# Attention feeding a two-layer FFN: tails loaded last, token order written into PSUM, zeros in early waits, casts in landing order

**Chip and metric.** One core of one Trainium2 chip. Times are device microseconds (us) of whole executions. Every run quoted fell in the same (fast) state. A run of one kernel spreads by about 1%.

## The reference, cut to what matters

```python
# q, k, v: (8 batches, 8 heads, 576 tokens, 64) fp32
scores = q @ k.T / 8, only where |query - key| <= 32, softmax over keys
x = (softmax @ v).transpose(0, 2, 1, 3).reshape(4608, 512)    # tokens x (heads*64)
out = gelu_tanh(x @ w_in) @ w_out                             # 512 -> 2048 -> 512
```

## The kernel before

Attention of one batch is woven between the matmuls of the feed-forward network of a block of 512 tokens. `ffn_in` is the input projection (`mm`/`ph <- xT,w_in` in the profile), then comes the output projection (`mm <- w_out,gT`). The heads of a pair sit on 64 partitions each. Queries are held four to a position: token 4p+j stands at column (j, p). So scores, weights and values come out with all tokens of j = 0 first, then j = 1 and so on, but the projection wants `xT` in token order, (p, j). A *group* is one pair of heads over 480 tokens of a batch (512 in batch 0); a fifth group holds the last tokens, the *tails*, of all pairs. The parts concerned, with cuts marked by "...":

```python
def weigh(b, g):                          # values and denominators of one group
    o = psO.tile([128, 512], FP32, name="ps_o")      # PSUM
    d = psO.tile([128, 512], FP32, name="ps_d")      # PSUM
    for i, (hf, pr, k0, c, p0, p1, off) in enumerate(todo):
        ...
        for w, bk in ((0, o), (1, d)):
            for h in range(2):            # the two heads of the pair
                nc.tensor.matmul(
                    bk[r0:r0 + 64, at:at + 4 * n].rearrange(
                        "d (j p) -> d j p", j=4)[:, :, p0 - q0:p1 - q0],
                    V[:, c, 2 * pr + h, :] if w == 0 else ones,
                    pes[hf][:, h, off:off + 4 * (p1 - p0)].rearrange("k (j p) -> k j p", j=4),
                    start=(i == 0), stop=(i == len(todo) - 1), ...)

def invert(b, g, d):                      # 1/denominator on ScalarE: exp(-ln d)
    nc.scalar.activation(lt[:, 0:n], d[:, 0:n], AF.Ln)
    nc.scalar.activation(lt[:, 0:n], lt[:, 0:n], AF.Exp, scale=-1.0)

def spread(b, g, o, lt):                  # the "product", on VectorE: token order is made here
    o4, l4 = (x[:, 0:n].rearrange("d (j p) -> d j p", j=4) for x in (o, lt))
    ...
    nc.vector.tensor_tensor(
        xT[:, g, pos:pos + 4 * e].rearrange("d (p j) -> d j p", j=4),   # fp16, step of 4 elements
        o4[:, :, p:p + e], l4[:, :, p:p + e], op=ALU.mult)

# loads of batch 1, in order: q,k of heads 0-1; q and k tails (tokens 512-575); q,k of heads 2-7;
# w_out 0, then halves of w_out 1-3 with v heads 0-5 between them (the v tail after v head 1), v heads 6-7
# casts on GpSimd while block 0 runs: w_out 1, v pairs 0 and 1, w_out 2, w_out 3, v pairs 2 and 3
# spin(n, width): matmuls of zeros, meant to keep TensorE's clock up; spin(4, 256) in the opening
```

The softmax here doesn't subtract the row's maximum and nothing guards it: scores larger than these inputs give would overflow.

## Time and profile before

| | before |
|---|---|
| timed median (3 runs first, 4 beside the changed kernel) | 329.77, 330.17 us |
| span of the profiled execution | 330.8 us |
| second input projection (block 1) starts | 67.96 us |
| from there to the end | 262.8 us |

Two views of the page of the kernel before follow. The first line gives each engine's busy time, its share of the span and its number of instructions. The second is the chain of work that ended last, by engine and line.

```profile
PE 314.4 (95%) x2244; PEld 152.4 (46%) x2244; DVE 149.2 (45%) x292; ACT 200.6 (61%) x314; POOL 57.5 (17%) x81
...
PE mm L445 37%; PE mm L432 22%; PE ph L432 13%; PE ps_o L377 4%; PE ps_s L344 4%; PE ps_d L377 3%; DMA KT<-k 2%; DMA vr<-in_v_dram 2%; DMA kr<-in_k_dram 2%; DVE xT L403 1%; SPq L123 1%; DVE pe L359 1%; SPq L132 1%; SPq L304 1%; ACT lt L392 1%
```

Nearly the whole chain is TensorE (PE). The value and denominator matmuls (`ps_o`, `ps_d`, L377) hold only 7% of it and the product (`xT`, L403, on DVE) 1%.

### The profile page before, as it was taken

The numbers are of one execution on the slowest core, as the hardware profiler recorded it, in microseconds if no ns is written. First come the engines' busy times: TensorE is split into PE (matmuls) and PEld (weight loads), VectorE is DVE, ScalarE is ACT, GpSimd is POOL, SyncE is SP. The second block draws the span as 40 slices with busy tenths as digits, with TensorE's granted clock in tenths as the row PEclk, the third lists the DMA queues.
The fourth block names the chain that finished last, engine by engine and source line by source line (L and its number), as shares of the span: only waits on it lengthen the run. The fifth ranks groups of instructions, "written<-read, shape, count | busy, mean of one in ns | idle before, by whom it ended". The sixth has DMA issues, their size and how long they took to land.

```text
span 330.8 us, 5704 instructions
## 1 busy us (share of the span) xinstructions
PE 314.4 (95%) x2244; PEld 152.4 (46%) x2244; DVE 149.2 (45%) x292; ACT 200.6 (61%) x314; POOL 57.5 (17%) x81
## 2 busy tenths in 40 slices
PE   7669987999999999999999999999999999999994
PEld 3543543544454445444544454445444554444441
DVE  5585575680468046814581457235632650210011
ACT  1476573467766677667767766685768567705600
POOL 3652345292104010401040104010000000000000
PEclk9698997999999999999999999999999999999999
DMA  7999999699979698979899899979161100020012
GB/s 196 275 361 303 329 316 292 175 155 152 231 179 141 122 205 170 124 134 206 176 103 135 179 218 91 152 191 208 65 119 26 65 37 28 0 95 34 0 63 63
DMA packets 119722, 50.57 MB, mean 153 GB/s; under 512 B 100144, under 2 KB 111152, under 8 KB 119696
## 3 DMA queue, kind: packets, MB, share of 16 engines
q1 hardware_dynamic: 88096, 45.10, 55.8%
q0 software_dynamic: 31520, 4.98, 20.0%
q8 instruction: 17, 0.28, 0.4%
q10 hardware_dynamic: 80, 0.13, 0.1%
q14 instruction: 9, 0.07, 0.1%
HBM read 37.62 MB, written 9.44 MB: 142 GB/s over the span
## 4 chain that ended last, share of the span: by engine, by line
PE 85%; DMA 5%; SPq 3%; DVE 3%; ACT 1%; POOL 1%; issue 1%; POOLq 0%
PE mm L445 37%; PE mm L432 22%; PE ph L432 13%; PE ps_o L377 4%; PE ps_s L344 4%; PE ps_d L377 3%; DMA KT<-k 2%; DMA vr<-in_v_dram 2%; DMA kr<-in_k_dram 2%; DVE xT L403 1%; SPq L123 1%; DVE pe L359 1%; SPq L132 1%; SPq L304 1%; ACT lt L392 1%
## 5 line engine op out<-in xcount | busy, mean ns | idle before, releaser
L445 PE MATMUL mm<-w_out,gT 128*128 128x512 f16 x576 | 134.9, 382 | 2.9 <-POOL w_out L183 2.2
L432 PE MATMUL mm<-xT,w_in 128*128 128x512 f16 x364 | 90.1, 382 | 1.3 <-DVE xT L403 1.3
L432 PEld LDWEIGHTS <-w_in 128*128 128x128 f16 x576 | 56.3, 98 | 69.6 <-issue 4.2
L445 PEld LDWEIGHTS <-gT 128*128 128x128 f16 x576 | 53.0, 98 | 66.5 <-issue 4.7
L436 ACT ACTIVATE gT<-mm 128x512 f16<-128x512 f32 x91 | 54.2, 597 | 38.4 <-PE mm L432 37.8
L403 DVE TENSOR_TENSOR xT<-ps_o,lt 128x480 f16<-128x480 f32 (+5 forms) x38 | 37.1, 1018 | 43.0 <-ACT lt L392 43.0
L432 PE MATMUL ph<-xT,w_in 128*128 128x512 f16 x212 | 55.9, 381 | 0.0
L391 ACT ACTIVATE lt<-ps_d 128x480 f32<-128x480 f32 (+3 forms) x40 | 22.2, 554 | 48.8 <-PE ps_d L377 48.7
L350 ACT ACTIVATE pe<-ps_s 128x704 f16<-128x704 f32 x64 | 43.3, 727 | 10.0 <-PE ps_s L344 9.0
L412 DVE TENSOR_TENSOR xT<-ps_o,lt 128x384 f16<-128x384 f32 (+1 forms) x8 | 7.9, 987 | 81.1 <-ACT lt L392 81.1
L449 DVE COPY yo<-mm 128x512 f32<-128x512 f32 x36 | 24.8, 690 | 34.1 <-PE mm L445 34.0
L436 ACT ACTIVATE gT<-ph 128x512 f16<-128x512 f32 x53 | 31.6, 596 | 13.0 <-PE ph L432 13.0
L359 DVE TENSOR_TENSOR pe<-pe,mask 128x704 f16<-128x704 f16 x64 | 33.1, 547 | 5.9 <-ACT pe L350 5.4
L163 POOL DMA_DIRECT2D V<-in_v_dram x24 | 23.2, 980 | 63.9 <-PE ps_o L377 47.6
L377 PEld LDWEIGHTS <-V 128*64 128x64 f16 x336 | 19.3, 114 | 18.7 <-issue 15.5
L392 ACT ACTIVATE lt<-lt 128x480 f32<-128x480 f32 (+3 forms) x40 | 23.5, 587 | 1.3
L377 PE MATMUL ps_d<-pe,ones 128*64 128x192 f16 (+2 forms) x264 | 23.8, 244 | 0.0
L377 PE MATMUL ps_o<-pe,V 128*64 128x160 f16 (+2 forms) x244 | 22.7, 248 | 0.7 <-DVE pe L359 0.4
L344 PE MATMUL ps_s<-QT,KT 64*128 64x192 f16 (+5 forms) x336 | 19.3, 232 | 2.3 <-ACT lt L392 1.1
L377 PEld LDWEIGHTS <-ones 128*64 128x64 f16 x336 | 19.7, 114 | 0.0
L165 POOL DMA_DIRECT2D V<-in_v_dram x6 | 5.5, 914 | 60.1 <-PE ps_d L377 46.7
L344 PEld LDWEIGHTS <-KT 64*128 64x128 f16 x336 | 11.1, 96 | 9.5 <-issue 3.4
(52 smaller groups left out, 147.5 us busy)
## 6 DMA issues: line engine op xcount, KB each, us to landing
kr<-in_k_dram SPq DMA_DIRECT2D x32, 256.0 KB, 7.3
out_dram<-yo SPq DMA_DIRECT2D x31, 256.0 KB, 2.8
qr<-in_q_dram SPq DMA_DIRECT2D x6, 1024.0 KB, 6.3
V<-in_v_dram POOLq DMA_DIRECT2D x30, 128.0 KB, 4.6
wst<-in_moe_w_in_dram SPq DMA_DIRECT2D x3, 1024.0 KB, 11.3
wst<-in_moe_w_out_dram SPq DMA_DIRECT2D x6, 512.0 KB, 7.7
qr<-in_q_dram SPq DMA_DIRECT2D x8, 256.0 KB, 5.5
vr<-in_v_dram SPq DMA_DIRECT2D x16, 128.0 KB, 5.4
```

Source lines behind the costliest of these rows:

```text
L163: nc.gpsimd.dma_start(V[:, c, :, :], v[b, :, 128 * c:128 * c + 128, :].rearrange("h p d -> p h d"))
L344: nc.tensor.matmul(ps[:, h, off:off + 4 * n].rearrange("k (j p) -> k j p", j=4), KTs[b % 2][r0:r0 + 64, pr, k0:k0 + 128], QTs[b][r0:r0 + 6 ...
L350: nc.scalar.activation(pe, ps[:, :, 0:w], AF.Exp, scale=SCALE)
L359: nc.vector.tensor_tensor(pe, pe, m.rearrange("p (o w) -> p o w", o=1).broadcast_to(list(pe.shape)), op=ALU.mult)
L377: nc.tensor.matmul(bk[r0:r0 + 64, at:at + 4 * n].rearrange("d (j p) -> d j p", j=4)[:, :, p0 - q0:p1 - q0], V[:, c, 2 * pr + h, :] if w == ...
L391: nc.scalar.activation(lt[:, 0:n], d[:, 0:n], AF.Ln)
L392: nc.scalar.activation(lt[:, 0:n], lt[:, 0:n], AF.Exp, scale=-1.0)
L403: nc.vector.tensor_tensor(xT[:, g, pos:pos + 4 * e].rearrange("d (p j) -> d j p", j=4), o4[:, :, p:p + e], l4[:, :, p:p + e], op=ALU.mult)
L432: nc.tensor.matmul(ph, w_in16[:, dc, fc * 128:fc * 128 + 128], xT[:, dc, t * 512 % RING:t * 512 % RING + 512], start=(dc == 0), stop=(dc = ...
L436: nc.scalar.activation(gTs[t][:, fc, :], ph, AF.Gelu_apprx_tanh)
L445: nc.tensor.matmul(py, gTs[t][:, fc, t4 * 128:t4 * 128 + 128], w_out16[:, fc, :], start=(fc == 0), stop=(fc == NF - 1))
L449: nc.vector.tensor_copy(yo, py)
```

## The change

Its intent has four parts. (1) *Tails last*: batch 1's tails wait behind everything that is needed sooner. (2) *Token order*: the value and denominator matmuls write PSUM in token order, so that the product on VectorE writes plainly too. (3) *Zeros*: more matmuls of zeros while TensorE waits in the opening, meant to keep its clock up. (4) *v casts*: GpSimd casts v heads between the w_out casts in the order in which they land. The full diff also moves some smaller steps of the same opening: pairs 1 and 2 of batch 1 are transposed a chunk earlier, batch 1's tails are cast and batch 2's rows are asked for behind the last w_out cast, and the tails' scores come at step 56 in place of 52. The diff, cut to its core:

```diff
 def weigh(b, g):
-    bk[r0:r0 + 64, at:at + 4 * n].rearrange(
-        "d (j p) -> d j p", j=4)[:, :, p0 - q0:p1 - q0],
+    bk[r0:r0 + 64, at + 4 * (p0 - q0):at + 4 * (p1 - q0)].rearrange(
+        "d (p j) -> d j p", j=4),

 def spread(b, g, o, lt):
-    nc.vector.tensor_tensor(xT[:, g, pos:pos + 4 * e].rearrange("d (p j) -> d j p", j=4),
-        o4[:, :, p:p + e], l4[:, :, p:p + e], op=ALU.mult)
+    nc.vector.tensor_tensor(xT[:, g, pos:pos + e], o[:, done:done + e],
+        lt[:, done:done + e], op=ALU.mult)
     (and the same for the tails' product)

-spin(4, 256)
+spin(3, 512)
+spin(2, 512)    (three times, between the first scores and transposes)

 loads of batch 1
-qk(0); tails(); qk(2); qk(4); qk(6) ... vs(1); vtail() ... vs(6, 7)
+qk(0); qk(2); qk(4); qk(6) ... vs(1) ... vs(6, 7); vtail(); tails()

 casts of batch 1, with w_out 1, 2, 3
-g == 1: cast_v(1, 0), cast_v(1, 1);  g == 3: cast_v(1, 2), cast_v(1, 3)
+g > 0:  cast_v(1, g - 1);            g == 3: cast_v(1, 3), cast_vt(1), cast_tails(1)
     (the tails' transposes move from the input projection to step 48 of the output projection)
```

More of the change, by code (lines that the diff above doesn't have):

```diff
@@ L40 @@
 PLAN = {3: ([-1], [0]), 14: ([], [1]), 24: ([0], [2]), 35: ([1], [3]), 46: ([2], [4]), 58: ([3], [])}
-TURN_0 = {9: [0], 12: [4, 1], 14: [2], 15: [3]}
+TURN_0 = {9: 0, 11: 1, 13: 2, 15: 3}
 PLAN_0 = {0: "w0 w1 m0", 14: "s1 m1", 16: "v0 s2 w2 x0 m2", 24: "v1 s3 w3 x1", 32: "m3 v2 s-1 x2 m-1",
-          42: "v3 x3", 52: "v-1 x-1 s4 m4"}
+          42: "v3 x3", 48: "t4", 52: "v-1 x-1", 56: "s4 m4"}
 ORDER_0 = ([(t4, 4 * w + i) for w in range(4) for t4 in (0, 1) for i in range(4)] +
@@ L246, in cast_early, with cast_vt @@
                             src[:, 2 * pr:2 * pr + 2, :].rearrange("p h (j d) -> p h j d", j=4))
+    def cast_vt(b):
+        n = 128 if b else 64
+        nc.gpsimd.tensor_copy(Vs[b % 2][0:n, 4, :, :], raws[b][4][0:n])
     def cast_v(b, pr):
-        vr, vt = raws[b][3:5]
+        vr = raws[b][3]
         hs = slice(2 * pr, 2 * pr + 2)
         nc.gpsimd.tensor_copy(Vs[b % 2][:, 0:4, hs, :], vr[:, :, hs, :])
-        if pr == 0:
-            n = 128 if b else 64
-            nc.gpsimd.tensor_copy(Vs[b % 2][0:n, 4, :, :], vt[0:n])
     def cast_tails(b, eng):
@@ L398, in spread @@
         if g < 4:
-            o4, l4 = (x[:, 0:n].rearrange("d (j p) -> d j p", j=4) for x in (o, lt))
-            pos, p = b * S % RING, 0
-            while p < n // 4:
-                e = min(n // 4 - p, (RING - pos) // 4)
-                nc.vector.tensor_tensor(
-                    xT[:, g, pos:pos + 4 * e].rearrange("d (p j) -> d j p", j=4),
-                    o4[:, :, p:p + e], l4[:, :, p:p + e], op=ALU.mult)
-                p, pos = p + e, (pos + 4 * e) % RING
+            pos, done = b * S % RING, 0
+            while done < n:
+                e = min(n - done, RING - pos)
+                nc.vector.tensor_tensor(xT[:, g, pos:pos + e], o[:, done:done + e],
+                                        lt[:, done:done + e], op=ALU.mult)
+                done, pos = done + e, (pos + e) % RING
         else:
-            w = n // NPAIR
             pos = (b * S + 4 * cut(b)) % RING
-            assert pos + w <= RING
-            o4, l4 = (x[:, 0:n].rearrange("d (r j p) -> d r j p", r=NPAIR, j=4) for x in (o, lt))
+            assert pos + n // NPAIR <= RING
             nc.vector.tensor_tensor(
-                xT[:, :, pos:pos + w].rearrange("d r (p j) -> d r j p", j=4), o4, l4, op=ALU.mult)
+                xT[:, :, pos:pos + n // NPAIR], o[:, 0:n].rearrange("d (r q) -> d r q", r=NPAIR),
+                lt[:, 0:n].rearrange("d (r q) -> d r q", r=NPAIR), op=ALU.mult)
     def values(b, g):
@@ L466 @@
     cast_v(0, 0)
+    cast_vt(0)
     cast_early(0, 2, both)
@@ L477 @@
     qk, tails, vs, vtail = load_early(1)
-    qk(0)
-    tails()
-    qk(2)
-    qk(4)
-    qk(6)
+    for h in range(0, H, 2):
+        qk(h)
     wo = [load_w_out(0, stage_w())]
@@ L495 @@
     score(0, 0)
+    spin(2, 512)
     pt = turn(1)
@@ L499 @@
     mask(0, 0, (1,))
+    spin(2, 512)
     score(0, 1)
+    spin(2, 512)
     pt = turn(2)
@@ L527 @@
     vs(1)
-    vtail()
     for i in (2, 3):
@@ L534 @@
     vs(6, 7)
+    vtail()
+    tails()
     cast_open(1)
@@ L541 @@
     pts = {}
-    cast_early(1, 0, (nc.gpsimd, nc.vector))
-    cast_tails(1, nc.gpsimd)
-    cast_early(1, 1, (nc.gpsimd, nc.vector))
+    split = (nc.gpsimd, nc.vector)
+    cast_early(1, 0, split)
+    cast_early(1, 1, split)
     for fc in range(2, NF):
-        for pr in TURN_0.get(fc, ()):
-            if pr == 4:
-                trans_tails(1, pts[0][:, 1, :, :])
-                continue
+        if fc in TURN_0:
+            pr = TURN_0[fc]
             if pr > 1:
-                cast_early(1, pr, (nc.gpsimd, nc.vector))
+                cast_early(1, pr, split)
             if pr < 2:
-                pts[pr] = psS.tile([128, 2, 8, 128], FP16, name="pt", tag=f"S{pr}")
-            trans_pair(1, pr, pts[0][:, 0] if pr == 0 else pts[1][:, pr - 1] if pr < 3 else
+                pt = psS.tile([128, 2, 8, 128], FP16, name="pt", tag=f"S{pr}")
+            trans_pair(1, pr, pt[:, pr // 2] if pr < 3 else
                        psO.tile([128, 8, 128], FP16, name="pt", tag="O"))
@@ L578 @@
             load_exp_table()
-        if b + 1 < B:
+        if t and b + 1 < B:
             load_qk(b + 1)
@@ L587 @@
                     cast_w(wo[g], w_out16[:, 4 * g:4 * g + 4, :])
-                    if g == 1:
-                        cast_v(1, 0)
-                        cast_v(1, 1)
-                    elif g == 3:
-                        cast_v(1, 2)
-                        cast_v(1, 3)
+                    if g:
+                        cast_v(1, g - 1)
+                    if g == 3:
+                        cast_v(1, 3)
+                        cast_vt(1)
+                        cast_tails(1, nc.gpsimd)
+                        load_qk(2)
+                elif kind == "t":
+                    pt = psS.tile([128, 2, 8, 128], FP16, name="pt", tag="S1")
+                    trans_tails(1, pt[:, 0])
                 elif kind == "s":
```

## The prediction

> **What bounds the kernel now.** I read the page first, then the table by stretches, then the timelines of TensorE (PE), GpSimd (POOL) and VectorE (DVE). The page has TensorE busy for 95% of 330.8 us. The table by stretches (per line: length; busy us of PE, PEld, DVE, ACT and POOL, each with its count; granted clock, DMA share, GB/s) says where the other 5% is:
>
> ```profile
> 8.00:16.00 8.00, 5.38 (x68) 3.91 (x66) 4.92 (x10) 3.56 (x6) 5.49 (x9) 0.66 1.16 271
> 16.00:24.00 8.00, 5.13 (x82) 3.92 (x81) 7.31 (x9) 6.30 (x10) 4.35 (x6) 0.92 1.07 355
> 24.00:32.00 8.00, 7.69 (x29) 3.05 (x29) 4.17 (x9) 5.66 (x10) 2.63 (x5) 0.79 1.12 312
> ...
> 48.00:56.00 8.00, 5.29 (x38) 2.39 (x35) 4.37 (x8) 2.83 (x6) 4.70 (x7) 0.79 1.14 315
> ...
> 68.00:101.60 33.60, 33.51 (x250) 16.18 (x249) 16.34 (x33) 22.23 (x37) 10.90 (x11) 1.00 1.30 174
> ```
>
> From 68 us on TensorE is busy in 33.51 of 33.60 us at full clock: there the order and length of its matmuls are the time, and a faster VectorE earns nothing. All idle time and all low clock lie before 68 us, while the DMA share is about 1: that part is fed by loads. The largest hole is where the first output projection waits for w_out. The timeline of TensorE (start, length, what, idle before it), then that of GpSimd:
>
> ```profile
> 48.62 0.71 PE L445 MATMUL mm<-w_out,gT 128*128 128x512 f16 x2 [0.53 <-DVE w_out L183]
> 51.07 0.38 PE L445 MATMUL mm<-w_out,gT 128*128 128x512 f16 x1 [1.74 <-POOL w_out L183]
> 51.88 2.29 PE L445 MATMUL mm<-w_out,gT 128*128 128x512 f16 x5 [0.44 <-POOL w_out L183]
> ```
>
> ```profile
> 49.47 0.61 POOL L251 CAST V<-vr 128x512 f16<-128x512 f32 x1 [2.61 <-DMA vr<-in_v_dram]
> 50.02 1.80 POOL L183 CAST w_out<-wst 128x512 f16<-128x512 f32 x2
> 52.84 1.17 POOL L183 CAST w_out<-wst 128x512 f16<-128x512 f32 x2 [1.01 <-DMA wst<-in_moe_w_out_dram]
> ```
>
> GpSimd stood 2.61 us before a V cast whose heads had not landed, with the next w_out cast behind it in its queue; TensorE stood 1.74 us for that cast. The five matmuls at 51.88 take 2.29 us, against 5 x 0.216 = 1.08 us where TensorE is warm.
>
> The groups by shape, from 68 us on (count, busy us, mean ns, idle before):
>
> ```profile
> L449 DVE COPY yo<-mm 128x512 f32<-128x512 f32 x33 | 22.7, 689 | 34.1 <-PE mm L445 34.0
> L403 DVE TENSOR_TENSOR xT<-ps_o,lt 128x480 f16<-128x480 f32 x16 | 19.7, 1232 | 24.3 <-ACT lt L392 24.3
> ```
>
> The product that puts tokens in order costs 1232 ns for 480 elements, the plain copy out of PSUM 689 ns for 512.
>
> [...] The trace has 1232[...]; the visible difference is the output, fp16 at a step of four elements. [...] The change makes the value and denominator matmuls write fp32 at a step of 16 bytes. No matmul of the kernel before writes so[...]. [...] in slices of one microsecond the clock is 0.50 from 11 to 17, 25 to 27 and 52 to 54 us, each time after a thin stretch. [...] about 190 to 210 GB/s at 29 to 31 us, where tails are in flight, against 385 for the weights at 24 to 26 us.
>
> **The change part by part.**
>
> *Tails last.* Batch 1's q and k tails (2 x 128 KB) no longer stand ahead of pairs 1 to 3, and the v tail (256 KB) no longer ahead of the last half of w_out. At some 200 GB/s, 0.26 MB is 1.3 us. So pairs 1 to 3 and w_out 0 and 1 land about 1.3 us earlier, w_out 2 and 3 and v heads 2 to 7 about 2.6 us earlier. Pair 0 of batch 1 lands as before (its k cast starts at 32.44 us, on its DMA).
>
> *v casts in landing order.* GpSimd now casts w1, v0, w2, v1, w3: w_out 2 no longer stands behind heads 2 and 3. With both parts its first cast can begin about 46.4 us instead of 50.02.
>
> *Zeros.* Six 512-wide matmuls are added between the first scores and three of 512 replace four of 256. Cold, one costs 0.43 us, warm 0.22. They lie where TensorE waited anyway (0.46, 1.12 and 0.80 us before the k cast, the KT copy and the q cast between 9.3 and 12.4 us), so I charge at most 0.3 us. If the clock then stays full, the work of 13.3 to 17.7 us, done cold in 4.1 us, takes about 2.2: up to 1.9 us.
>
> *Token order.* The same matmuls at the same count; the product falls from 1.30 to about 0.69 us in the opening (512 elements), 1.23 to 0.66 later. From 16 to 24 us VectorE is busy 7.3 of 8, and two such products are on its path to the first input projection (19.0 to 26.1 us): 2 x 0.6 = 1.2 us. From 68 us on: nothing.
>
> *Sum up to the input projection.* It starts in earnest at 26.07 us; minus 1.9, minus about 0.6 to 1.2, plus 0.3: about 24 us. But it can't keep this: seven chunks later (7 x 0.864 = 6.0 us) TensorE reaches the transposes of pair 0, which have to wait for the k cast that ends at 32.9 us. Before, they ran at 33.28. So about 0.4 us of 2 remain; the rest is lost to a load.
>
> *From there on.* Chunks 9 to 15 are 7 x 0.864 = 6.05 us, four transposed pairs 4 x 0.45 = 1.8; with pairs 1 to 3 landed in time that ends at 32.9 + 7.85 = 40.8, before 42.08. The tail transposes (0.22 us) only move.
>
> *The first output projection.* It starts near 41.2. Its matmuls 0 to 15 with the scores and values between them fill to about 46.2, w_out 2 is cast by 47.6, so matmul 23 ends at 48.6 (before: 54.1); w_out 3 lands near 50.2 instead of 52.84, and matmul 31 ends near 52.4 (before: 57.4). Then 32 x 0.216 = 6.9 us, four value and score blocks of 2.2 us and about 0.5 us of small waits: near 62.0 us, before 67.96. **Gain: 6.0 us**; 2.7 us of it are the three waits shown, about 1.3 us the cold clock behind them, the rest is the earlier start and smaller waits.
>
> *What is given back.* The same bytes must still land. Batch 2's rows come behind the tails, and its transposes were just in time before:
>
> ```profile
> 83.20 0.26 PEld L344 LDWEIGHTS <-KT 64*128 64x128 f16 x8 [0.23 <-DMA KT<-k]
> ```
>
> TensorE would arrive there near 77.2 us. VectorE's casts of batch 2 started right after the last copy of the first projection (68.77 us, no wait for a load), so they mostly move along, but the loads end only around 64 us. I give back 1 us. From there 246.6 us are unchanged. **330.8 - 6 + 1 = 325.8 us in the profile; the timed median is 1 us below the span, so 325 us.**
>
> **The rivals.** *A, strided writes slow the matmuls.* Value and denominator matmuls stream, per pair of heads, 736 columns a group in batch 0 and 672 later, four groups, twice, plus 768 for tails: 6656 + 7 x 6144 = 49,664 columns[...], nearly all in the stretch that TensorE bounds. TensorE's timeline shows this at full rate today:
>
> ```profile
> 88.90 0.25 PE L377 MATMUL ps_o<-pe,V 128*64 128x192 f16 x2
> 88.99 0.25 PE L377 MATMUL ps_d<-pe,ones 128*64 128x192 f16 x2
> 89.07 0.25 PE L377 MATMUL ps_o<-pe,V 128*64 128x192 f16 x2
> ```
>
> Pairs of 192 columns follow each other at 80 to 90 ns[...]. At half rate the cost is about 20 us: 345 us. [...] Against it: [...] VectorE reads PSUM at a 256-byte step in the KT copy in 680 ns, its ordinary rate; and someone who tuned this closely would have seen 20 us. I give A 28%. *B, the loads take it all.* If DMA merely reorders, the wait moves to batch 2's transposes near 77 us and 4 to 5 us are given back: 329 us. For it: DMA share about 1 up to 58 us. Against: the DMA is nearly idle from 64 to 66 us (15 GB/s), so there is slack. *C, it goes better.* The opening keeps its 2 us because pair 0, too, lands earlier without the tails, and nothing is given back: 322 us.
>
> **Range and chances.** Without A I expect 325 with some 2.5 us to either side; 2% is 6.6 us, a line at 323.2, so about a third of that case is faster by over 2%. With A 343 to 347. The time is two-humped and I take the more probable hump, but the range must reach over the other: 320 to 347. Faster 0.25, same 0.47, slower 0.28.
>
> **What would show it.** Right: the product at about 660 ns for 480; value matmuls of 192 columns still 80 ns apart; no wait for w_out over 0.7 us near 47 to 52 us and no clock of 0.5 there; a wait of one or two us before pair 0's transposes near 31 us; the second input projection starting near 62 us; TensorE saturated afterwards, 33.5 us a token block. Wrong: value matmuls of 192 columns 160 ns apart and blocks of some 36 us (A); a wait for KT of several us near 77 (B); product still at 1.2 us (then the output step was not its cause).

The product's 0.69 and 0.66 us: the changed kernel shows them (690 ns for 512 elements, 658 for 480; the plain copy of 512 takes 689 in the kernel before). That zeros hold the clock was an expectation; the trace shows only that TensorE was busy 0.56, 1.00 and 0.33 us in the two microseconds from 9, 22 and 49 us, around the end of which the clock fell to 0.50. Of rival A, its 49,664 columns: at the 82 ns that 192 columns take in the trio, those columns take 21 us (an estimate), and at half rate as much again: so the "about 20 us" and the 345 us stand.

## The result, and the profile after

Ratios here and below are the mean time of one kernel's fast runs over the mean of the other's of the same rounds, so not quite the ratio of the quoted medians. The changed kernel took **342.50 us** (342.31 to 343.76), against 330.17 us (329.52 to 330.92) for the kernel before: a ratio of 1.038 (95% interval 1.0345 to 1.0416), slower.

The same two views of the page of the changed kernel:

```profile
PE 329.6 (97%) x2249; PEld 166.4 (49%) x2249; DVE 137.6 (40%) x292; ACT 200.7 (59%) x314; POOL 57.8 (17%) x81
...
PE mm L443 38%; PE mm L430 22%; PE ph L430 13%; PE ps_o L378 7%; PE ps_d L378 6%; PE ps_s L345 4%; DMA vr<-in_v_dram 2%; PE mm L378 1%; SPq L123 1%; PE pt L276 0%; DVE xT L403 0%; DVE KT L282 0%; ACT lt L393 0%; PE pt L274 0%; ACT lt L392 0%
```

VectorE is 11.6 us less busy and TensorE 15.2 us more, with five more matmul records (nine zeros in place of four). The product is all but gone from the chain, and `ps_o` and `ps_d` have gone from 7% of it to 13%. Next is TensorE's timeline (start, length, what, idle before it) in a value group of block 1, to be held against the trio at 88.90 us in the prediction:

```profile
85.25 0.37 PE L378 MATMUL ps_o<-pe,V 128*64 128x192 f16 x2
85.42 0.37 PE L378 MATMUL ps_d<-pe,ones 128*64 128x192 f16 x2
85.58 0.37 PE L378 MATMUL ps_o<-pe,V 128*64 128x192 f16 x2
```

The two heads' matmuls of 192 columns now follow the previous pair after 163 ns on average, where it was 82. That is 0.85 ns for a column in place of 0.43; below, 0.43 ns (82 ns for 192 columns) is called one cycle, so each column takes two instead of one. It is the same where the granted clock is 0.50 (160 and 320 ns). The timeline of the kernel before in the opening, then that of the changed kernel (`mm` is here a PSUM bank that the values of every second group of batch 0 borrow):

```profile
14.09 0.37 PE L377 MATMUL mm<-pe,V 128*64 128x192 f16 x2
14.25 0.37 PE L377 MATMUL ps_d<-pe,ones 128*64 128x192 f16 x2
14.41 0.37 PE L377 MATMUL mm<-pe,V 128*64 128x192 f16 x2
```

```profile
13.68 0.61 PE L378 MATMUL mm<-pe,V 128*64 128x192 f16 x2
14.00 0.61 PE L378 MATMUL ps_d<-pe,ones 128*64 128x192 f16 x2
14.32 0.61 PE L378 MATMUL mm<-pe,V 128*64 128x192 f16 x2
```

160 ns became 320 ns: at the granted clock of 0.50 the slow clock did not hide the cost, it doubled both figures (82 and 163 ns at 1.00). That the clock was low here in both, and so that the zeros did not keep it up in this execution of the changed kernel, is seen in the stretch from 14 to 16 us, of the kernel before and then of the changed one (the last three columns are clock, DMA share and GB/s):

```profile
14.00:16.00 2.00, 2.00 (x32) 1.81 (x30) 1.43 (x3) 0.64 (x2) 1.63 (x3) 0.50 1.14 299
14.00:16.00 2.00, 2.00 (x20) 1.73 (x18) 0.93 (x2) 0.07 (x1) 1.34 (x3) 0.50 1.11 309
```

The other parts can be seen further on. From the changed kernel, in this order: two stretches (length; busy us of PE, PEld, DVE, ACT and POOL with counts; clock, DMA share, GB/s); the output projection on TensorE; w_out's cast on GpSimd; the product by shape.

```profile
48.00:56.00 8.00, 8.00 (x78) 4.50 (x77) 6.71 (x11) 4.95 (x9) 5.66 (x8) 1.00 0.98 229
68.00:104.00 36.00, 36.00 (x250) 18.12 (x249) 15.31 (x37) 23.51 (x38) 8.18 (x8) 1.00 1.31 164
```

```profile
47.27 2.00 PE L443 MATMUL mm<-w_out,gT 128*128 128x512 f16 x8 [0.70 <-DVE w_out L183]
```

```profile
44.67 1.46 POOL L183 CAST w_out<-wst 128x512 f16<-128x512 f32 x2 [1.74 <-DMA wst<-in_moe_w_out_dram]
```

```profile
L403 DVE TENSOR_TENSOR xT<-ps_o,lt 128x480 f16<-128x480 f32 x16 | 10.5, 658 | 36.0 <-ACT lt L393 36.0
```

From 48 to 56 us TensorE has no idle time where it had 2.71 us, and the clock is full where it was 0.79. The slow stretch of the loads went with the tails: from 29 to 31 us the DMA moved 347 GB/s where it had moved 200, and the low is now at 48 to 52 us (194, then 107 GB/s), where the tails are in flight. The product takes 658 ns. But the second input projection starts at 64.10 us, 3.9 us sooner than before, and the rest takes 276.7 us, 13.9 us longer.

A batch has four groups of 1344 columns, 672 of values and 672 of denominators. At 81 ns more for 192 columns (163 less 82) one more cycle per column is 0.57 us a group (estimate), and a group took 0.70 us before and 1.26 us after, so 0.56 more. The tails (768 columns, estimate 0.32 us more, from the same 81 ns) went from 0.53 to 0.81 us. Together that is 4 x 0.56 + 0.28 = 2.52 us. Block 1, with four groups and one batch's tails, went from 33.62 to 35.98 us, and each of the five blocks after it from 33.71 to 35.97: 2.36 and 2.26 us, the rest of the 2.52 being small waits that the kernel before had in these blocks and the changed one has not. So 2.36 + 5 x 2.26 + 0.17 for the last tails is 13.8 us of the 13.9.

### The profile page after: what moved, and what is told of

It is laid out like the page before. It is cut to its first block, busy times and chain, and to the rows that moved or that the text cites. A ratio compares the mean times of both kernels' runs of the same rounds, so it can differ in the third digit from the quotient of the medians.

```text
span 340.8 us, 5712 instructions
## 1 busy us (share of the span) xinstructions
PE 329.6 (97%) x2249; PEld 166.4 (49%) x2249; DVE 137.6 (40%) x292; ACT 200.7 (59%) x314; POOL 57.8 (17%) x81
## 4 chain that ended last, share of the span: by engine, by line
PE 92%; DVE 2%; DMA 2%; SPq 1%; ACT 1%; POOL 1%; issue 0%; POOLq 0%
PE mm L443 38%; PE mm L430 22%; PE ph L430 13%; PE ps_o L378 7%; PE ps_d L378 6%; PE ps_s L345 4%; DMA vr<-in_v_dram 2%; PE mm L378 1%; SPq L123 1%; PE pt L276 0%; DVE xT L403 0%; DVE KT L282 0%; ACT lt L393 0%; PE pt L274 0%; ACT lt L392 0%
## 5 line engine op out<-in xcount | busy, mean ns | idle before, releaser
L430 PE MATMUL mm<-xT,w_in 128*128 128x512 f16 x364 | 89.0, 379 | 1.1 <-DVE xT L403 1.0
L403 DVE TENSOR_TENSOR xT<-ps_o,lt 128x480 f16<-128x480 f32 (+5 forms) x38 | 20.3, 552 | 59.1 <-ACT lt L393 59.1
L378 PE MATMUL ps_d<-pe,ones 128*64 128x192 f16 (+2 forms) x264 | 40.3, 351 | 0.0
L360 DVE TENSOR_TENSOR pe<-pe,mask 128x704 f16<-128x704 f16 x64 | 35.6, 559 | 8.7 <-ACT pe L351 6.3
L409 DVE TENSOR_TENSOR xT<-ps_o,lt 128x384 f16<-128x384 f32 (+1 forms) x8 | 4.3, 541 | 83.4 <-ACT lt L393 83.4
L378 PE MATMUL ps_o<-pe,V 128*64 128x160 f16 (+2 forms) x244 | 37.1, 342 | 0.0
L378 PEld LDWEIGHTS <-V 128*64 128x64 f16 x336 | 24.3, 140 | 16.6 <-issue 12.3
L378 PEld LDWEIGHTS <-ones 128*64 128x64 f16 x336 | 24.9, 143 | 0.7
L345 PE MATMUL ps_s<-QT,KT 64*128 64x192 f16 (+5 forms) x336 | 18.2, 229 | 1.8 <-DVE KT L282 1.8
```

The lines of the kernel that those rows point to most:

```text
L345: nc.tensor.matmul(ps[:, h, off:off + 4 * n].rearrange("k (j p) -> k j p", j=4), KTs[b % 2][r0:r0 + 64, pr, k0:k0 + 128], QTs[b][r0:r0 + 6 ...
L360: nc.vector.tensor_tensor(pe, pe, m.rearrange("p (o w) -> p o w", o=1).broadcast_to(list(pe.shape)), op=ALU.mult)
L378: nc.tensor.matmul(bk[r0:r0 + 64, at + 4 * (p0 - q0):at + 4 * (p1 - q0)].rearrange("d (p j) -> d j p", j=4), V[:, c, 2 * pr + h, :] if w = ...
L403: nc.vector.tensor_tensor(xT[:, g, pos:pos + e], o[:, done:done + e], lt[:, done:done + e], op=ALU.mult)
L430: nc.tensor.matmul(ph, w_in16[:, dc, fc * 128:fc * 128 + 128], xT[:, dc, t * 512 % RING:t * 512 % RING + 512], start=(dc == 0), stop=(dc = ...
```

## The experiments

The theory: a PSUM write at a step of 16 bytes costs TensorE two cycles per column (the prediction's rival A), and the other parts gain a little. The rivals: a lost gain at the loads, a cost of zeros or of the moved casts, or a cost from anything else that changed around the matmuls. Twelve kernels ran, all correct, with 3 rounds each unless noted.

### 1 and 2: the one part undone, and the one part alone

`a_not_token` is the changed kernel with the write of `weigh` and the product of `spread` as before. `b_token_only` is the kernel before with only these two changed.

```diff
 a_not_token (against the changed kernel)
-    bk[...at + 4 * (p0 - q0):at + 4 * (p1 - q0)].rearrange("d (p j) -> d j p", j=4),
+    bk[...].rearrange("d (j p) -> d j p", j=4)[:, :, p0 - q0:p1 - q0],
     and spread() of the kernel before
 b_token_only (against the kernel before): the same lines, the other way round
```

> The changed kernel with its token order undone: values and denominators written plainly into PSUM, the product writes at a step of four again; zeros, tails last and v casts stay. Theory 1 (each column that a matmul writes at a 16-byte step costs TensorE two cycles in place of one): 342.5 - 13.9 (the growth of everything after the second input projection starts, 276.7 us against 262.8) - 2 to 4 (the same cost in the first two batches) = 325 to 327 us, and pairs of 192 columns 80 ns apart again. Rival R (the growth has another cause: the zeros, weight loads, the other order of loads): it stays near 340.

> The kernel before with nothing but the token order in PSUM and the plain product. Theory 1: 330.2 + 13.9 + 1 to 4 in the first two batches = 345 to 348 us; product near 0.65 us for 480 elements. Rival R: 329 to 331.

Measured, beside 330.66 us for the kernel before in the same rounds: `a_not_token` **327.34 us** (ratio 0.990, 0.985 to 0.995), `b_token_only` **345.01 us** (1.042, 1.038 to 1.047). TensorE's timeline of `a_not_token`, the trio of a value group:

```profile
83.22 0.25 PE L378 MATMUL ps_o<-pe,V 128*64 128x192 f16 x2
83.30 0.25 PE L378 MATMUL ps_d<-pe,ones 128*64 128x192 f16 x2
83.39 0.25 PE L378 MATMUL ps_o<-pe,V 128*64 128x192 f16 x2
```

Where the second input projection starts, and what is left from there, sort the four kernels:

| profiled run | 2nd projection starts | from there to the end |
|---|---|---|
| before | 67.96 us | 262.8 us |
| `b_token_only` | 66.67 us | 276.7 us |
| changed | 64.10 us | 276.7 us |
| `a_not_token` | 62.29 us | 262.9 us |

The right column has two values only, and the PSUM order decides which. The token order costs about 15 us: 15.2 by the two medians (342.50 less 327.34, of different rounds), 15.6 by the profiled spans, 14.4 on the kernel before in the same rounds (345.01 less 330.66). It is the whole loss and more. Without it the change gains 1%.

### 3 and 7: make the token order elsewhere

If PSUM must be written plainly, the order can be made by reading. `c_read_order` lets the product read both inputs in token order and write `xT` plainly. `f_act_order` lets ScalarE read the denominators in token order in its logarithm, so that the product has only one stepped input, in PSUM.

```diff
 c_read_order (against a_not_token)
-    o4, l4 = "d (j p) -> d j p";   xT written as "d (p j) -> d j p"
+    o4, l4 = "d (j p) -> d p j";   xT written as "d (p j) -> d p j"   (plain)
 f_act_order (against c_read_order)
-    nc.scalar.activation(lt[:, 0:n], d[:, 0:n], AF.Ln)
+    nc.scalar.activation(lt as "d (p j) -> d p j", d as "d (j p) -> d p j", AF.Ln)   # lt plain
```

> The changed kernel, but values stay plain in PSUM, and the product walks its two inputs in token order (steps of 480 bytes in PSUM and SBUF) and writes xT without a step. If only the stepped 2-byte output made the product slow, it takes about 0.65 us for 480 and the kernel 323 to 326 us, below both. If stepped inputs cost the same, the product stays at 1.2 us or more and the kernel is as in the run with token order undone, 325 to 327.

> As the run in which the product reads in token order, but ScalarE writes the inverse sums in token order (its logarithm reads PSUM at a step of 480 bytes), so the product has one stepped input left, in PSUM. If the stepped SBUF input was what kept that product at 986 ns: about 660 ns and 1 us or so off 326.2, 324.5 to 326.5, with the logarithm still near 570 ns. If the PSUM input was: it stays near 986 ns.

Measured: `c_read_order` **326.21 us** (0.986, 0.981 to 0.991), `f_act_order` **326.40 us** beside 330.35 (0.988, 0.984 to 0.992). The product in groups by shape (count, busy us, mean ns, idle before), of `c_read_order` and then of `f_act_order`:

```profile
L404 DVE TENSOR_TENSOR xT<-ps_o,lt 128x480 f16<-128x480 f32 x16 | 15.8, 986 | 26.1 <-ACT lt L393 26.1
```

```profile
L410 DVE TENSOR_TENSOR xT<-ps_o,lt 128x480 f16<-128x480 f32 x16 | 10.5, 657 | 27.7 <-ACT lt L398 27.7
```

VectorE read PSUM at a step of 480 bytes at its plain rate (657 ns, against 658 in the changed kernel). The same step on the fp32 input in SBUF as well cost half as much again (986 ns). ScalarE's logarithm stayed at 570 ns (571 in the changed kernel) with its PSUM input at that step. So here the order can be had for nothing in the reads of PSUM, and the product is as fast as the change wanted. Yet the time is that of `a_not_token` within the intervals: VectorE was hardly what the end waits for. The trace shows a little: each later block takes 33.6 us in both kernels, 33.7 in `a_not_token`, some 0.6 us in all.

### 4: step the moving operand instead

`d_moving_order` streams the weights in token order from SBUF, so that the PSUM write is plain again, to ask whether the order of the stream or the write costs.

```diff
-    bk[...].rearrange("d (p j) -> d j p", j=4),   pes[...].rearrange("k (j p) -> k j p", j=4)
+    bk[...].rearrange("d (p j) -> d p j", j=4),   pes[...].rearrange("k (j p) -> k p j", j=4)
```

> The changed kernel, but each value and denominator matmul reads its moving operand in token order (fp16 at a step of 64 to 96 bytes) and writes PSUM plainly. If only the stepped write costs TensorE: value pairs of 192 at 80 ns, 323 to 326 us. If a stepped read costs it as well: pairs at 160 ns or more and 340 us or more. I expect the second, at 0.65.

Measured: **384.17 us** (1.161). TensorE's timeline:

```profile
95.67 0.51 PE L378 MATMUL ps_o<-pe,V 128*64 128x192 f16 x2
96.00 0.51 PE L378 MATMUL ps_d<-pe,ones 128*64 128x192 f16 x2
96.32 0.51 PE L378 MATMUL ps_o<-pe,V 128*64 128x192 f16 x2
```

325 ns a pair: four cycles per column for fp16 read at a step of 64 to 96 bytes. Both the stepped write and the stepped read cost, and the read more (325 ns against 163).

### 5 and 6: which step costs

Two forms of the write lie between plain and the change's. `e_pairs8` streams and writes two consecutive columns next to each other (8 bytes), then steps by 32 bytes. `g_step8` writes single fp32 values at a step of 8 bytes. If what costs is that two consecutive columns don't share 8 bytes, the first is free and the second as dear as the change. If any step costs, both are dear. If the cost grows with the step, `g_step8` is cheaper than the change.

```diff
 e_pairs8 (against the changed kernel; the product reads "d (a j b) -> d a b j")
-    bk[...] as "d (p j) -> d j p",  pes[...] as "k (j p) -> k j p"
+    bk[...] as "d (a j b) -> d j a b", b=2,  pes[...] as "k (j a b) -> k j a b"
 g_step8 (the product writes runs of two fp16)
+    bk[...] as "d (i p j) -> d i j p", i=2, j=2
```

> The changed kernel, but each value or denominator matmul writes runs of two neighbouring fp32 (8 bytes) at a step of 32 bytes; the product reads them at steps of 8 and 32 bytes and writes xT without a step. If what costs is that two columns in a row don't share 8 bytes (theory 1a): pairs of 192 columns 80 ns apart, some 324 to 327 us. If any stepped write costs two cycles (1b): 163 ns and 340 to 344 us; something between if it is counted by runs.

> The changed kernel, but the matmuls write at a step of 8 bytes in place of 16 (two of the four token offsets interleaved); the product writes xT in runs of two. Theory 1a (8 bytes shared or not): no two columns in a row share 8 bytes, so pairs of 192 stay at 163 ns and the kernel at 340 to 344 us. Theory 1c (only steps of 16 bytes or more cost): 80 ns, 324 to 328 us. I hold 1a at 0.7.

Measured, beside 330.35 us: `e_pairs8` **327.72 us** (0.991, 0.987 to 0.996), `g_step8` **342.88 us** (1.037, 1.034 to 1.041). TensorE's timeline of `e_pairs8`, then of `g_step8`:

```profile
85.02 0.25 PE L378 MATMUL ps_o<-pe,V 128*64 128x192 f16 x2
85.11 0.25 PE L378 MATMUL ps_d<-pe,ones 128*64 128x192 f16 x2
85.19 0.25 PE L378 MATMUL ps_o<-pe,V 128*64 128x192 f16 x2
```

```profile
85.09 0.37 PE L378 MATMUL ps_o<-pe,V 128*64 128x192 f16 x2
85.26 0.37 PE L378 MATMUL ps_d<-pe,ones 128*64 128x192 f16 x2
85.42 0.37 PE L378 MATMUL ps_o<-pe,V 128*64 128x192 f16 x2
```

82 ns against 163 ns, with nothing between. In these runs the price does not go by whether the write is contiguous (82 ns for plain writes and for runs of two at a step of 32 bytes), nor by how wide the step is (163 ns at 8 and at 16 bytes), but by whether two consecutive columns go into the same 8 bytes. Why is not shown. The product of `g_step8`, which writes runs of two fp16, took 657 ns for 480 elements, as in the changed kernel. All pairs of `e_pairs8` start at a multiple of 8 bytes; whether a pair that doesn't is as cheap was not tried.

### 11: is the cost additive?

`n_half` is `f_act_order` with only the values, not the denominators, written at the 16-byte step.

```diff
-    bk[...] as "d (j p) -> d j p"
+    bk[...] as "d (p j) -> d j p" if w == 0 else "d (j p) -> d j p"
```

> As the run in which ScalarE reorders the denominators (326.4 us), but the values, and only they, are written at the 16-byte step. Half the columns at two cycles: values pairs of 192 at 163 ns, denominator pairs at 80, and half of 16.1 (342.5 - 326.4), so 326.4 + 8 = 334.5 us (333.5 to 335.5). If the cost were not additive by columns (for instance a price for the switch), it is away from that.

Measured: **333.97 us** beside 330.46 (1.009, 1.006 to 1.013), 7.6 us over `f_act_order`. One pair of each kind took 245 ns together, the sum of the 163 and 82 ns measured above. The cost went by the column here, so it can be reckoned.

### 8, 9 and 10: the zeros and the v casts

`i_no_zeros` is `a_not_token` with the spins of the kernel before. `j_zeros_only` is the kernel before with only the new spins (5 rounds). `m_old_casts` is `i_no_zeros` with the old order of the v casts (5 rounds).

```diff
 i_no_zeros (against a_not_token)          j_zeros_only (against before): the reverse
-spin(3, 512)                              m_old_casts (against i_no_zeros)
+spin(4, 256)                              -if g: cast_v(1, g - 1)
-spin(2, 512)   (three times)              +if g == 1: cast_v(1, 0); cast_v(1, 1)
                                           +if g == 3: cast_v(1, 2)   (ahead of cast_v(1, 3))
```

> The run with token order undone (327.3 us), and the added zeros taken away as well, so that of the change only the late tails and the v casts in landing order are left. If the zeros earn through the clock: the clock is 0.5 again in part of 10 to 17 us, the first output projection begins about where it did with the zeros or up to 1 us later, since pair 0's rows of batch 1 bound it: 327.5 to 329 us. If the gain of the whole rest is the zeros': 330.

> The kernel before with nothing but the zeros (three of 512 for four of 256, and six more). The clock should be 1.0 in 10 to 17 us, and the first input projection start up to 2 us earlier; but the w_out wait near 50 us is set by loads, so it takes most of that back: 329 to 330.5 us against 330.4, ratio 0.995 to 1.0. If the zeros earn their whole opening gain: 328.

> The run with the zeros taken away (328.8 us), with the v casts in their old order as well, so that of the change only the late tails are left. If the casts' order earns what my prediction said, the w_out 2 cast of GpSimd waits for heads 2 and 3 again (idle near 1 to 2 us ahead of a V cast, TensorE waits for w_out on GpSimd): 329 to 330.5 us. If the late tails alone did it: 328.5 to 329.

| kernel | median us | before, same rounds | ratio (95%) |
|---|---|---|---|
| `a_not_token` | 327.34 | 330.66 | 0.990 (0.985 to 0.995) |
| `i_no_zeros` | 328.80 | 330.35 | 0.995 (0.991 to 0.999) |
| `m_old_casts` | 328.60 | 330.46 | 0.994 (0.990 to 0.998) |
| `j_zeros_only` | 331.19 | 330.46 | 1.001 (0.998 to 1.004) |

In `a_not_token` the clock stayed up with the zeros. The table by stretches of `i_no_zeros`, then of `a_not_token`:

```profile
12.00:16.00 4.00, 3.04 (x38) 2.41 (x36) 2.01 (x4) 1.57 (x3) 3.20 (x6) 0.50 1.05 297
```

```profile
12.00:16.00 4.00, 3.04 (x63) 2.57 (x64) 2.56 (x5) 2.22 (x4) 2.85 (x6) 1.00 1.15 305
```

The granted clock from 12 to 16 us goes from 0.50 to 1.00, and TensorE does 63 matmuls instead of 38 in the same 3.04 us. They don't always: of the ten profiled kernels with the new zeros seven kept a clock of 1.00 from 12 to 18 us, while it fell to 0.50 for about 3 us or more in the changed kernel, `d_moving_order` and `n_half`. Why is not shown; in the four kernels without the new zeros it was 0.50 for most of that time. And alone, on the kernel before, they earn nothing: the input projection waits for its data at 26 us as it did, and the w_out wait stays. TensorE's timeline of `j_zeros_only`:

```profile
26.20 0.59 PE L432 MATMUL mm<-xT,w_in 128*128 128x512 f16 x2 [1.20 <-DVE xT L403]
...
50.79 0.58 PE L445 MATMUL mm<-w_out,gT 128*128 128x512 f16 x1 [1.88 <-POOL w_out L183]
```

`m_old_casts` shows the v casts to be worth nothing that can be seen. GpSimd again waits 2.49 us for v, and its w_out cast comes behind that, but TensorE then waits for VectorE's half of the cast, and about as long either way. GpSimd and then TensorE in `m_old_casts`, then TensorE in `i_no_zeros`:

```profile
45.62 0.62 POOL L255 CAST V<-vr 128x512 f16<-128x512 f32 x1 [2.49 <-DMA vr<-in_v_dram]
```

```profile
47.38 0.38 PE L446 MATMUL mm<-w_out,gT 128*128 128x512 f16 x1 [1.31 <-DVE w_out L183]
```

```profile
47.82 0.38 PE L446 MATMUL mm<-w_out,gT 128*128 128x512 f16 x1 [1.20 <-DVE w_out L183]
```

So by the means, of the 1% that the change gains without its token order somewhat over half comes with the late tails (`m_old_casts`, which has besides them only the smaller moved steps), and the remainder with zeros on top of late tails. The intervals of these kernels overlap, so the division is not settled.

### 12: is there more to be had?

In `f_act_order` TensorE waits 2.4 us for VectorE's casts of w_out, 1.7 us of it for w_out 2. `o_early_w2` starts that cast two steps earlier (5 rounds).

```diff
-14: "s1 m1",    16: "v0 s2 w2 x0 m2"
+14: "s1 w2 m1", 16: "v0 s2 x0 m2"
```

> As the run in which ScalarE reorders the denominators (326.4 us), with VectorE's casts of the third w_out block ahead of the second group's masks, so that TensorE's wait of 1.36 + 0.37 us for them near 48 us goes. If nothing takes its place: 324.7 to 325.4 us. If the wait for batch 2's transposes (0.6 us there) grows by as much: 326 to 326.5.

Measured: **326.61 us** beside 330.46 (0.990, 0.985 to 0.995), no gain over `f_act_order` (0.988). The waits of `f_act_order`, then of `o_early_w2` (engine and line, releaser, us in total, times, longest):

```profile
PE mm L453 <- DVE w_out L183: 2.4, 4, 1.4
PE ps_s L345 <- DMA KT<-k: 0.6, 1, 0.6
PE mm L453 <- POOL w_out L183: 0.9, 2, 0.8
```

```profile
PE ps_s L345 <- DMA KT<-k: 1.2, 1, 1.2
PE mm L453 <- POOL w_out L183: 1.2, 4, 0.5
PE mm L453 <- DVE w_out L183: 0.2, 1, 0.2
```

The wait was taken away, and 0.9 us came back in the two others: TensorE was sooner at batch 2's first scores and waited longer for KT there. Where the rest went can't be told from these two profiles, since that of `f_act_order` (327.91 us) is the slowest of its runs and that of `o_early_w2` (326.08 us) the fastest of its own. `c_read_order` at 326.21 us has the best time of all. It is 1.4% faster than the kernel before and 4.8% faster than the change (326.21 / 342.50, of different rounds), but it can't be told from `f_act_order` or `o_early_w2`.

## Why the prediction was wrong

**The step that failed** is *Token order*, in the words "The same matmuls at the same count" and "From 68 us on: nothing." The count was right and the cost per matmul was not: two cycles per column instead of one. That stretch went from 262.8 to 276.7 us. Rival A named this, with its size (20 us, total 345), and was given 28%; the measured 342.50 us lie just below its 343 to 347. Of the arguments against it that stand, that VectorE reads PSUM at a 256-byte step "in 680 ns, its ordinary rate", was true and beside the point: experiment 7 shows VectorE and ScalarE reading PSUM at a step of 480 bytes for nothing (657 and 570 ns), in the kernel family in which TensorE pays double for writing it at 8 or 16 (163 against 82 ns). The other, that someone who tuned this closely would have seen it, was no argument from the trace. The kernel before has no matmul that writes at a step, so nothing measured spoke against A, and a pair of 82 ns on a saturated engine made the stake some 20 us. Nor did its trace show A to be the likelier case: the 28% was the author's estimate, and only an experiment could have settled it.

**The size of A**, about 20 us, was about 15. On the spans (340.8 less 325.2, so 15.6) two terms make the difference. At 81 ns more for 192 columns all 49,664 would cost 21.0 us (an estimate, as are the next two sizes). After the start of the second input projection come 37,632 columns, or 15.9 us; they cost 13.8 (276.7 less 262.9), mostly because the longer matmuls cover small waits. And 12,032 columns or 5.1 us (batch 0, and batch 1 but for its tails) lie before that, where TensorE often waits: only 1.8 us of them showed (64.10 against 62.29), the lower clock in this execution of the changed kernel included. 21.0 - 2.1 - 3.3 = 15.6.

**The rest, without A**, was predicted at 325 and is `a_not_token`: 327.3. Step by step:

- *The product*: predicted 660 ns for 480, measured 658 (1232 before). Right, and so is its cause: a whole group's inputs were read plainly before too, so that only the stepped 2-byte output went. At the end it is worth some 0.6 us (experiments 3 and 7), less than the medians can tell.
- *Second projection starts near 62.0*: 62.29 in `a_not_token`. Right, but partly by luck: two of its terms, pair 0 and the v casts, were wrong (below), and in the other kernels with all parts and 82 ns per pair (`c_read_order`, `e_pairs8`, `f_act_order`, `o_early_w2`) it started between 61.02 and 63.51. And before to `a_not_token` differ by 5.6 us in span and only 3.3 us in the medians. "The timed median is 1 us below the span" held for this pair of figures only because the page is that of a slow execution: the time of an execution lies 1.7 us above its own span (332.54 against 330.8). The gain of 6 us was measured from a bad sample.
- *Pair 0 of batch 1 lands as before* was wrong, harmlessly. GpSimd's timeline shows its q cast, of the kernel before and then of the changed one:

```profile
31.66 0.61 POOL L245 CAST q<-qr 128x512 f16<-128x512 f32 x1 [5.00 <-DMA qr<-in_q_dram]
```

```profile
29.45 0.70 POOL L245 CAST q<-qr 128x512 f16<-128x512 f32 x1 [3.99 <-DMA qr<-in_q_dram]
```

  It came 2.2 us sooner, and no wait stood before its transposes. The prediction's own reading, 190 to 210 GB/s while tails are in flight, was right and pointed this way: without the tails the DMA moved 347 at that time.
- *v casts*: predicted as a part of the 3.6 us by which GpSimd's w_out cast comes sooner. `m_old_casts` shows no gain from it.
- *Zeros*: predicted up to 1.9 us of which 0.4 remain. Alone they gave 0 (1.001); on late tails perhaps 1.5 us, not settled. In the changed kernel itself the clock was 0.50 from 14 to 16 us in spite of them.
- *Given back*, 1 us at batch 2's transposes: the wait for KT is absent in the changed kernel and in `a_not_token`, 0.6 in `f_act_order`, 1.2 in `o_early_w2`, 1.5 in `e_pairs8`. Right in kind, and about right in size where it came. Rival B (4 to 5 us taken by that wait) is out: the longest such wait is 1.5 us, and `a_not_token` has none.
- *Slips that decide nothing*: "246.6 us are unchanged" should be 247.6 (330.8 less 83.2). And 3.7 us of TensorE's idle time lie after 135 us, so not all of it before 68.

What stays open: how the remaining 1% divides between late tails, zeros and the smaller moved steps, which the intervals don't separate, and why the zeros kept the clock up in some kernels and not in others.

## What to carry to other kernels

Before moving a layout change from an idle engine into a matmul's output, look at two consecutive columns of the stream: where they didn't share 8 bytes of PSUM here, the matmul took twice as long (163 against 82 ns for 192 columns), and if TensorE is the bound that is the end of the idea. Put the order where reading was free here instead (VectorE or ScalarE out of PSUM, 657 and 570 ns at a step of 480 bytes), or keep runs of two in the write (82 ns). And when a cost of unknown size may fall on the saturated engine, price it in full and argue against it only with a measurement of the same operation.
